# Block-sparse attention with an MLP behind it: the queues that carry P through DRAM

## The chip, the cores and the metric

The kernel runs on one core of a Trainium2 chip. The metric is the device time of one execution in microseconds, lower is better. The kernel before was timed three times: the median is 821.48 us (818.59 to 822.83).

## What is computed

Attention over 4 batches, 8 heads, 768 positions and head size 64, in blocks of 32 positions. A query block sees its neighbours, the first and the last block and three sampled blocks; the first and the last query block see everything. The heads are then joined to rows of 512 and pass a two-layer MLP.

```python
scores = scale * np.matmul(q, k.transpose(0, 1, 3, 2))
scores = np.where(mask, scores, -1000000000.0)
attn = np.exp(scores - np.max(scores, axis=-1, keepdims=True))
attn = attn / (np.sum(attn, axis=-1, keepdims=True) + 1e-09)
x = np.matmul(attn, v)            # [B, H, S, D] -> [B * S, H * D]
h = x @ w_in                      # 3072 x 512 by 512 x 2048
return (h * (1.0 / (1.0 + np.exp(-1.702 * h)))) @ w_out
```

## The kernel before

Tokens go through in six chunks of 512. The MLP of a chunk runs in 16 ticks, one for each 128 columns of the hidden layer (`tick`, L800). A tick holds the first product (`up`, L613: lines 624 to 626), the gate (`gate`, L629: tanh on ScalarE in line 632, a product on VectorE in line 641), its split into a high and a low part (line 648 on ScalarE, line 656 on VectorE) and the second product of the tick before (`down`, L659: lines 682, 686, 687). While one chunk's MLP runs, the attention of the next chunk is done in the gaps. The second weight lies split in DRAM (`ws`); each tick `stream` (L597) loads one piece of it through SyncE into one of two `wst` buffers (line 601), and `split` (L603) makes its two parts by a cast on ScalarE (line 606) and a subtraction on VectorE (line 607).

Attention is cut into items. A sparse item is two query blocks of all heads; a dense item is half of the heads against half of the keys of the first and last query block. `plan` (L740) places each item on quarters of ticks: its scores at one quarter (lines 306 or 318 on TensorE, the minimum in line 329 on VectorE, the exponentials in line 344 on ScalarE), its product with the values later (line 413 for sparse, 435 for dense items). In the sparse stretches some 15 quarters lie between the two, in the dense ones 8, and dense items follow each other every 4 quarters.

For the product with the values P has to be turned. 42 items (28 sparse, 14 dense) are marked `moved`: their exponentials stay in PSUM, VectorE turns them in squares of 32 into the only `ex` buffer (`turned_blocks`, line 356, two instructions), and `move` (L359) brings the squares to their places: one DMA from `ex` to one of two DRAM buffers `way` (line 365), and four DMAs from there to a `raw` buffer (line 367), each 32 partitions. The reads wait for the landing of the write. `pop` (L372) runs these three steps, either inside `gate`, just ahead of line 641, or at the end of a tick, just ahead of `split`.

Each engine issues its DMAs in the order in which the program writes them, and an instruction that waits holds what is behind it on that engine. SyncE issues nearly all of them: query and key loads (lines 206 to 218; the sampled key blocks in line 229, each with its block number read into a register first, line 228), values (lines 236 to 253), the weight pieces (line 601), the output (line 712) and P's five. GpSimd issues the gathers of sampled values (line 258) and, in the first chunk, the raw weights (line 517). ScalarE issues next to none.

Of the kernel before, what the change touches and what calls it, by code (L numbers as in the profile page):

```python
# [20 lines left out]
BLK = 32  # L21
# [29 lines left out]
class Kernel:  # L51
# [307 lines left out]
    def move(self, g):  # L359

        nt = 4 if self.sparse(g) else 3
        n = 2 * nt * BLK
        to = self.work.tile([P, 2 * DM], I32, name="raw", bufs=3).bitcast(F32)[:, 0:4 * n].rearrange("p (c f) -> p c f", c=4)
        way = self.way[g["n"] % 2][:, 0:4 * n]
        self.nc.sync.dma_start(out=way, in_=g["st"])
        for r in range(4):
            self.nc.sync.dma_start(out=to[BLK * r:BLK * (r + 1)],  # L367
                                   in_=way[:, n * r:n * (r + 1)].rearrange("(c i) f -> i c f", c=4))
        pt = to.rearrange("p c (h k j) -> p h k c j", h=2, k=nt)
        g["pt"] = [pt[:, h] for h in range(2)]  # L370

# [628 lines left out]
```

## Time and profile before

| | |
|---|---|
| median of three runs | 821.48 us (818.59 to 822.83) |
| the profiled execution, its own time | 815.69 us |
| its span | 813.9 us |
| TensorE (PE) busy | 723.9 us, 89% |
| VectorE (DVE) busy | 450.4 us, 55% |
| ScalarE (ACT) busy | 341.1 us, 42% |
| GpSimd (POOL) busy | 69.8 us, 9% |
| DMA engines, SyncE's queue | 49.9% of 16 engines' span |
| DMA engines, GpSimd's queue | 14.9% |

All times are of one execution. The first chunk's attention fills the span up to some 160 us, ticks with moved items run from 160 to 704 us, and the last chunk's MLP stands alone behind that. Busy time of TensorE includes products that run at the lower of its two clock levels. An engine's wait is named by what ended last. Times after an instruction's start are its duration; a DMA has besides a time from its issue to its landing.

### The profile page before, as it was taken

The numbers are of one execution on the slowest core, as the hardware profiler recorded it, in microseconds if no ns is written. First come the engines' busy times: TensorE is split into PE (matmuls) and PEld (weight loads), VectorE is DVE, ScalarE is ACT, GpSimd is POOL, SyncE is SP. The second block draws the span as 40 slices with busy tenths as digits, with TensorE's granted clock in tenths as the row PEclk, the third lists the DMA queues.
The fourth block names the chain that finished last, engine by engine and source line by source line (L and its number), as shares of the span: only waits on it lengthen the run. The fifth ranks groups of instructions, "written<-read, shape, count | busy, mean of one in ns | idle before, by whom it ended". The sixth has DMA issues, their size and how long they took to land.

```text
span 813.9 us, 19176 instructions
## 1 busy us (share of the span) xinstructions
PE 723.9 (89%) x7452; PEld 542.8 (67%) x7452; DVE 450.4 (55%) x1153; ACT 341.1 (42%) x855; POOL 69.8 (9%) x111
## 2 busy tenths in 40 slices
PE   3879999999797978979988888899896999999997
PEld 2665667766575746757666666667574767788885
DVE  4669888985563544535643636544564647443332
ACT  4656666754242423423433425233442434333322
POOL 5323211011000001000000000100000000000000
PEclk9999999999898989989999998999998999999999
DMA  8999976767776669676766466666667766441111
GB/s 259 283 370 375 323 268 237 246 198 231 215 242 201 184 202 266 199 203 212 225 203 207 123 191 214 212 197 214 198 195 252 248 193 195 138 103 40 52 52 52
DMA packets 94492, 167.28 MB, mean 206 GB/s; under 512 B 10977, under 2 KB 55266, under 8 KB 93890
## 3 DMA queue, kind: packets, MB, share of 16 engines
q1 hardware_dynamic: 82162, 124.10, 49.9%
q0 software_dynamic: 11376, 41.03, 14.9%
q8 instruction: 59, 0.97, 0.5%
q10 hardware_dynamic: 864, 0.93, 0.3%
q14 instruction: 31, 0.25, 0.1%
HBM read 135.34 MB, written 30.67 MB: 204 GB/s over the span
## 4 chain that ended last, share of the span: by engine, by line
PE 42%; DMA 20%; SPq 14%; DVE 11%; ACT 7%; issue 6%; ACTq 0%; DVEq 0%
DMA way<-ex 10%; PE bank L624 6%; DMA wst<-ws 6%; PE bank L625 6%; PE bank L626 6%; PE bank L682 4%; PE bank L686 4%; PE bank L687 4%; ACT bank L344 4%; SPq L228 4%; SPq L229 3%; PE bank L671 3%; PE bank L306 3%; SPq L367 2%; PE bank L413 2%
## 5 line engine op out<-in xcount | busy, mean ns | idle before, releaser
L686 PE MATMUL bank<-wout,ghi 128*128 128x512 f32 x352 | 139.0, 395 | 0.0
L687 PE MATMUL bank<-wout,ghi 128*128 128x512 f32 x352 | 137.1, 390 | 0.0
L607 DVE TENSOR_TENSOR wout<-wst,wout 128x512 fp32r<-128x512 f32 x80 | 55.1, 688 | 137.6 <-ACT wout L606 136.2
L632 ACT ACTIVATE g<-bank 128x512 f32<-128x512 f32 x96 | 57.5, 599 | 142.0 <-PE bank L626 142.0
L682 PE MATMUL bank<-wout,glo 128*128 128x512 f32 x352 | 100.3, 399 | 17.2 <-DVE glo L656 17.1
L641 DVE SCALAR_TENSOR_TENSOR g<-g,bank 128x512 f32<-128x512 f32 x83 | 56.1, 676 | 89.1 <-ACT g L632 89.0
L344 ACT ACTIVATE bank<-bank,nm 128x256 f32<-128x256 f32 (+1 forms) x140 | 65.3, 467 | 94.3 <-DVE nm L329 89.0
L648 ACT CAST ghi<-g 128x512 fp32r<-128x512 f32 x88 | 54.4, 618 | 97.6 <-DVE g L641 97.6
L624 PE MATMUL bank<-x,win 128*128 128x512 f32 x192 | 80.9, 421 | 14.2 <-DVE g L641 14.2
L624 PE MATMUL bank<-xhi,win 128*128 128x512 f32 x192 | 80.9, 421 | 11.3 <-DVE g L641 10.7
L682 PEld LDWEIGHTS bank<-wout,glo 128*128 128x128 f32 x352 | 66.3, 191 | 35.0 <-DVE glo L656 20.6
L329 DVE CUSTOM_DVE_ANT_1 bank<-bank,bias 128x256 f32<-128x256 f32 x176 | 73.6, 440 | 21.1 <-PE bank L306 14.5
L625 PE MATMUL bank<-x,win 128*128 128x512 f32 x192 | 78.0, 406 | 0.0
L626 PE MATMUL bank<-x,win 128*128 128x512 f32 x192 | 77.7, 405 | 0.0
L258 POOL DMA_INDIRECT vown<-in_v_dram,vidx x40 | 39.8, 994 | 433.9 <-PE bank L413 309.4
L625 PE MATMUL bank<-xlo,win 128*128 128x512 f32 x192 | 76.5, 398 | 0.0
L626 PE MATMUL bank<-xhi,win 128*128 128x512 f32 x192 | 76.4, 398 | 0.0
L686 PEld LDWEIGHTS bank<-wout,ghi 128*128 128x128 f32 x352 | 66.2, 188 | 13.8
L687 PEld LDWEIGHTS bank<-wout,ghi 128*128 128x128 f32 x352 | 66.2, 188 | 13.4
L606 ACT CAST wout<-wst 128x512 fp32r<-128x512 f32 x80 | 49.3, 616 | 59.5 <-DMA wst<-ws 59.5
L356 DVE STREAM_TRANSPOSE ex<-bank 128x512 f32<-128x512 f32 (+1 forms) x84 | 51.8, 651 | 35.8 <-DMA way<-ex 33.4
L306 PE MATMUL bank<-kg,qt 64*32 64x256 f32 x1280 | 49.3, 414 | 12.8 <-DMA vmid<-in_v_dram 11.5
(151 smaller groups left out, 1030.6 us busy)
## 6 DMA issues: line engine op xcount, KB each, us to landing
wst<-ws SPq DMA_DIRECT2D x80, 256.0 KB, 3.2
kg<-in_kb_dram SPq DMA_DIRECT2D x114, 128.0 KB, 2.7
way<-ex SPq DMA_DIRECT2D x28, 512.0 KB, 4.0
raw<-way SPq DMA_DIRECT2D x112, 128.0 KB, 2.9
kg<-in_kb_dram SPq DMA_DIRECT2D x42, 256.0 KB, 4.5
win<-in_moe_w_in_dram POOLq DMA_DIRECT2D x16, 512.0 KB, 7.4
raw<-in_moe_w_out_dram POOLq DMA_DIRECT2D x16, 512.0 KB, 5.9
kg<-in_kT_dram SPq DMA_DIRECT2D x4, 1536.0 KB
```

Of the source, the lines that this page charges most:

```text
L306: nc.tensor.matmul(sps[h][BLK * c:BLK * (c + 1), n * i:n * (i + 1)].rearrange("p (g n s) -> p g n s", g=2, s=BLK), self.qt[r][rows, bi, UT ...
L329: nc.vector.tensor_tensor_reduce(out=at, in0=at, in1=bias, scale=-SCALE, scalar=3.0e38, op0=ALU.add, op1=ALU.min, accum_out=un["nm"][:, ha ...
L344: nc.scalar.activation(out=ex, in_=sps[h][:, n * k:n * (k + 1)], func=AF.Exp, bias=un["nm"][:, half, c:c + 1], scale=-1.0, accum_out=un["r ...
L607: self.nc.vector.tensor_tensor(out=t[:, DM:2 * DM], in0=w, in1=t[:, 0:DM].bitcast(F32), op=ALU.subtract)
L624: nc.tensor.matmul(to, wih[:, k], xh, start=(k == 0), stop=False)
L625: nc.tensor.matmul(to, wih[:, k], xl, start=False, stop=False)
L626: nc.tensor.matmul(to, wil[:, k], xh, start=False, stop=(k == NCT - 1))
L632: nc.scalar.activation(out=g, in_=self.h, func=AF.Tanh, scale=0.851)
L641: nc.vector.scalar_tensor_tensor(out=g, in0=g, scalar=1.0, in1=h, op0=ALU.add, op1=ALU.mult)
L682: nc.tensor.matmul(to[n], glo[:, tk[n]], woh, start=False, stop=last)
L686: nc.tensor.matmul(to[n], ghi[:, tk[n]], woh, start=(f == 0), stop=False)
L687: nc.tensor.matmul(to[n], ghi[:, tk[n]], wol, start=False, stop=False)
```

## The change

The DMA from `ex` to `way` is issued by ScalarE, and the four from `way` to `raw` by GpSimd. Sizes, buffers and the place in the program stay.

```diff
         way = self.way[g["n"] % 2][:, 0:4 * n]
-        self.nc.sync.dma_start(out=way, in_=g["st"])
+        self.nc.scalar.dma_start(out=way, in_=g["st"])
         for r in range(4):
-            self.nc.sync.dma_start(out=to[BLK * r:BLK * (r + 1)],
-                                   in_=way[:, n * r:n * (r + 1)].rearrange("(c i) f -> i c f", c=4))
+            self.nc.gpsimd.dma_start(out=to[BLK * r:BLK * (r + 1)],
+                                     in_=way[:, n * r:n * (r + 1)].rearrange("(c i) f -> i c f", c=4))
```

On SyncE, behind the stores of a finished chunk, the order changes in this way (`out` is the output, `ws` and `wst` the weight pieces, `qt` and `kg` queries and keys):

```order
 L712 DMA out_dram<-raw 64x512 x4
 L712 DMA out_dram<-a 64x512 x4
-L365 DMA way_85<-ex 128x1024
-L367 DMA raw<-way_85 32x4x256 x4
 L601 DMA wst<-ws_72 128x512
 L601 DMA wst<-ws_73 128x512
-L365 DMA way_86<-ex 128x1024
-L367 DMA raw<-way_86 32x4x256 x4
 L206 DMA qt_105<-in_qd_dram 128x256
 L207 DMA kg_103<-in_kT_dram 128x3072
```

P's five DMAs no longer stand between the stores, the weight pieces and the next keys, and no wait for P's landing does.

On ScalarE, at the same place, the changed kernel has these rows in a row:

```order
L726 ACTIVATE a<-bank_92 128x512
L365 DMA way_85<-ex 128x1024
L606 CAST wout<-wst 128x512
L632 ACTIVATE g<-bank_94 128x512
L648 CAST ghi<-g 128x512
L606 CAST wout<-wst 128x512
L344 ACTIVATE bank_87,rs<-bank_87,nm 128x256 x2
L344 ACTIVATE bank_88,rs<-bank_88,nm 128x256 x2
L491 CAST xhi_110<-bank_89 128x4x64
L632 ACTIVATE g<-bank_94 128x512
L365 DMA way_86<-ex 128x1024
L648 CAST ghi<-g 128x512
```

The write stands once ahead of the cast of a weight piece (a `pop` at a tick's end) and once between tanh and the cast of the gate (a `pop` inside `gate`). Of the 42 writes 27 stand ahead of line 648, 8 ahead of line 606, 4 ahead of line 491 (the cast of the turned attention output), 2 ahead of line 452 (the dense items' factors) and 1 ahead of line 539.

On GpSimd, from the last raw weight on, the reads take turns with the gathers (`vown`):

```order
L517 DMA raw<-in_moe_w_out_dram 128x1024
L367 DMA raw<-way_85 32x4x256 x4
L258 DMA vown_107<-in_v_dram,vidx 128x1024 x2
L367 DMA raw<-way_86 32x4x256 x4
L367 DMA raw<-way_85 32x4x256 x4
L367 DMA raw<-way_86 32x4x256 x4
L258 DMA vown_106<-in_v_dram,vidx 128x1024 x2
```

Before, the gathers stood there alone; a gather now waits behind reads that wait for a write's landing.

## Rows read from the trace of the kernel before

**Rows 1.** Waits of TensorE, 160 to 704 us (us in total, times, longest)

```profile
PE bank L624 <- DVE g L641: 24.9, 12, 6.2
PE bank L682 <- DVE glo L656: 17.1, 6, 6.1
PE bank L435 <- DMA raw<-way: 8.0, 5, 2.8
PE bank L318 <- DVE ex L356: 7.5, 2, 4.7
PE bank L484 <- DVE x L492: 2.3, 1, 2.3
```

**Rows 2.** The first of these by stretch: 160 to 320, 320 to 600, 600 to 710 us

```profile
PE bank L624 <- DVE g L641: 8.8, 3, 5.8
...
PE bank L624 <- DVE g L641: 9.3, 7, 3.5
...
PE bank L624 <- DVE g L641: 6.8, 2, 6.2
```

**Rows 3.** Waits in SyncE's queue, 160 to 710 us, the longest

```profile
SPq L367 <- DMA way<-ex: 191.2, 42, 11.1
```

**Rows 4.** Waits of ScalarE, 160 to 710 us, the one for weights

```profile
ACT wout L606 <- DMA wst<-ws: 59.5, 14, 11.0
```

**Rows 5.** Timelines of SyncE and TensorE, a late weight piece (start, duration, instruction, idle before)

```profile
338.17 1.75 SPq L367 DMA_DIRECT2D raw<-way  x4
...
342.15 6.38 SPq L229 DMA_DIRECT2D kg<-in_kb_dram  x6
...
354.02 2.01 SPq L601 DMA_DIRECT2D wst<-ws  x2
...
361.41 2.08 PE L682 MATMUL bank<-wout,glo 128*128 128x512 f32 x4 [5.71 <-DVE glo L656]
```

**Rows 6.** Timelines of SyncE, VectorE and TensorE, a late write of P

```profile
199.88 0.56 SPq L365 DMA_DIRECT2D way<-ex  x1
...
205.46 1.31 DVE L356 STREAM_TRANSPOSE ex<-bank 128x512 f32<-128x512 f32 x2 [3.89 <-DMA way<-ex]
...
207.40 0.79 PE L624 MATMUL bank<-x,win 128*128 128x512 f32 x1 [5.84 <-DVE g L641]
```

**Rows 7.** Windows: PE, PEld, DVE, ACT, POOL busy (instructions), TensorE clock, DMA share, GB/s

```profile
160.00:704.00 544.00, 480.74 (x5155) 359.66 (x5154) 286.61 (x735) 208.63 (x538) 25.50 (x26) 0.95 0.68 208
206.00:208.00 2.00, 0.60 (x2) 0.51 (x3) 1.35 (x3) 0.62 (x1) 0.00 (x0) 0.50 0.65 189
```

**Rows 8.** Timelines of TensorE and VectorE, dense items 640 to 697 us

```profile
640.52 0.88 PE L318 MATMUL bank<-kg,qt 64*64 64x384 f32 x8
...
644.19 1.04 DVE L356 STREAM_TRANSPOSE ex<-bank 128x384 f32<-128x384 f32 x2
...
696.00 0.88 PE L318 MATMUL bank<-kg,qt 64*64 64x384 f32 x8
```

**Rows 9.** Lines 229 and 258: issue on GpSimd and ScalarE (duration ns min/median/max, starts)

```profile
L229 ACTq DMA_DIRECT2D kg<-in_kb_dram x3: 354/355/378, 3.1 to 5.3; - x3
...
L229 POOL DMA_DIRECT2D kg<-in_kb_dram x3: 536/571/727, 5.0 to 7.4; - x3
...
L258 POOL DMA_INDIRECT vown<-in_v_dram,vidx x40: 933/939/1438, 12.3 to 605.6; - x40
```

**Rows 10.** DMA issues: engine, count, KB each, median us to landing

```profile
way<-ex SPq DMA_DIRECT2D x28, 512.0 KB, 4.0
raw<-way SPq DMA_DIRECT2D x112, 128.0 KB, 2.9
...
kg<-in_kb_dram POOLq DMA_DIRECT2D x3, 128.0 KB, 4.2
...
wout<-in_kb_dram POOLq DMA_DIRECT2D x3, 128.0 KB, 8.9
```

**Rows 11.** Costliest groups: gate product (busy us, mean ns, idle before, releaser)

```profile
L641 DVE SCALAR_TENSOR_TENSOR g<-g,bank 128x512 f32<-128x512 f32 x83 | 56.1, 676 | 89.1 <-ACT g L632 89.0
```

## The prediction

> **What bounds the kernel now.** I read the waits of TensorE first. From 160 to 704 us it is busy for 480.74 of 544 us [rows 7], so 63.3 us are waits, and five rows hold 59.8 of them [rows 1] (two of under 2.5 us are left out there: another wait for the turned attention output, one for an exponential). None names the DMA queues except the 8.0 us of dense items for `raw`, so the next views are the timelines behind the longest waits, to see what made VectorE late. There are two patterns.
>
> *A weight piece comes late.* SyncE issues P's reads until 339.92 us, then six sampled key blocks, then a finished chunk's stores, and only at 354.02 the weight piece; the cast, the subtraction and the low part of the gate follow it, and TensorE stands for 5.71 us [rows 5]. ScalarE waited 59.5 us in 14 such places [rows 4]. To this I count the waits for line 656 but two of 1 us (17.1 - 2 = 15), for line 492 (2.3 and its like of 2.2, [rows 1]) and the longest of the middle stretch for line 641 (3.5, [rows 2]): **23 us**.
>
> *P's write comes late.* Line 356 may not overwrite `ex` before the last write has left it. At 199.88 us that write is issued behind a chunk's stores, the next turning waits 3.89 us for it, line 641 stands behind that, and TensorE behind line 641 for 5.84 us [rows 6]. With it go its like of 6.2 us in the last stretch [rows 2] and the two waits for line 356, 7.5 us [rows 1]: **19.5 us**.
>
> The reads themselves make 8.0 us [rows 1]. The rest, 63.3 - 23 - 19.5 - 8.0 = 12.8 us, are waits of 1 to 2 us for an item's own chain (scores, exponentials, turning, line 641); no queue is in it.
>
> Behind both patterns stands SyncE: it waits 191.2 us in 42 moves for P's landing [rows 3], 4.55 us each, and everything behind it waits too.
>
> **The change part by part.**
>
> *Off SyncE.* Each move takes 4.55 us of waiting, 1.75 us for four reads [rows 5] and 0.4 to 0.56 us for the write [rows 6]: 6.7 us, 42 times, 281 of 544 us. A piece that was late by what TensorE then waited (at most 6.1 us, [rows 1]) comes 6.7 us earlier where one move stood ahead of it. So I take 20 of the 23 us as gone; where keys and stores together still fill the two ticks for which a `wst` buffer lasts, the wait stays: bounds 10 to 23.
>
> *The write on ScalarE's queue.* It leaves when the turning ends, not behind stores or keys, and lands on a queue that holds nothing else. Of the 19.5 us the four places keep what the item's own chain costs elsewhere, some 1.3 us each: 14.3 us gone, bounds 8 and 19.5.
>
> *What it costs ScalarE.* The issue is 0.355 us on that queue [rows 9], and ScalarE stands until line 356 has ended. In 27 of 42 places the next instruction is the cast of line 648, which waits for line 641 anyway, and that one comes behind line 356 on VectorE and takes 0.676 us [rows 11]: the wait and the issue lie beside it and cost nothing. If line 641 came first, the cover would be gone and each of the 27 would cost up to 1.04 us of turning [rows 8] and the issue. In the other 15 places a cast or factor that could go at once is held for up to 1.04 + 0.36 + 0.2 us (the 0.2 for handing over, my estimate from 1.75 us for four issues of SyncE [rows 5], whose gaps are smaller): 24 us at most, 0 at least, since ScalarE is busy for 208.63 of 544 us [rows 7]. I take a third, 8 us, because the instruction that follows on VectorE stands behind the turning too, and only the cast's own time comes on top.
>
> *What it costs GpSimd.* 168 issues by 0.571 us [rows 9] are 96 us on an engine that is busy for 25.50 of 544 us [rows 7]. Gathers stand behind reads, by a write's landing of 4.0 us [rows 10] and 2.3 us of issues; they fill a buffer that is used only after two more items, some 30 quarters, which hides it. Without that cover it would be 6 us for each of the gathers' pairs.
>
> *The reads' landing.* No row shows a read of `way` by GpSimd. From below 2.9 us, as by SyncE, from above 8.9 us, a 128 KB load by GpSimd in the crowded prelude; 4.2 us is another of the same size there [rows 10]. I take 5, near the lower of GpSimd's own rows, for traffic in the stage is thinner. It counts in the dense stretches only: sparse items have 15 quarters. There items follow each other by (696.00 - 640.52) / 7 = 7.9 us, and an item's values come two items later, behind the scores of that one: 2 x 7.9 + 0.9 = 16.7 us [rows 8]. Its chain is 4.7 us to the end of the turning (645.23 - 640.52, [rows 8]), 0.4 for the issue, 4.0 for the write, 2.3 for four issues on GpSimd, 5 for the landing: 16.4 us. It just fits. Each us more would cost half a us for each of 14 dense items. So I leave the 8.0 us where they are: a write that leaves earlier and reads that take longer. Bounds: a gain of 8, or (8.9 - 5) / 2 x 14 = 27 us lost.
>
> The Trainium skill ("DMA: Bandwidth & Descriptors", section "Latency and other measured facts") puts the first byte at about 1 us on GpSimd's path against 0.6 on the other: by that the reads would land at about 3.3 us, and the dense items would gain a little instead.
>
> *The clock.* It falls to half, 1.2 GHz, behind long waits (0.50 in 206 to 208 us, [rows 7], with the wait of [rows 6] ahead of it). A mean of 0.95 over 544 us [rows 7] is 2 x 0.05 x 544 = 54 us at the lower level. Where TensorE worked in that time, half of it is lost; with a third of it spent waiting (in 206 to 208 it is 70%, later less, an estimate) that is 18 us. The two patterns are 42.5 of 63.3 us and hold all long waits, so I take 13 back: bounds 0 and 25.
>
> *The sum*: -20 - 14.3 + 8 - 13 = **-39 us**. The profiled execution took 815.69 us; it would take 776.4. The median of the three runs is 5.8 us above that execution, so I predict 821.48 - 39 = **782 us**. A measurement of this kernel can tell some 0.5% from no change, 4.1 us.
>
> **The rivals.**
>
> *The waits only change their name* (chance 0.17). With weights and writes in time, TensorE runs into each item's own chain, which stands in DVE's and ACT's order whatever the queues do. For it speaks that 12.8 us of such waits are there now and that the long ones hide others. If each of 42 moves then waits 0.6 us more than now, 25 us come back: 39 - 25 = 14, about **807 us**. Against it: at 640 to 697 us, where SyncE has no keys to load, items run at 7.9 us with hardly a wait [rows 8].
>
> *The queues are not the point* (0.09). If P's landing is bounded by the engines that move it, another queue only saves issue time on SyncE, 42 x 2.2 = 92 us that lie beside other work: no gain, **821 us**. For it: the DMA share is 0.68 over the stage [rows 7]. Against it: SyncE's wait, not the issue, is the larger part [rows 3], and key loads and stores stand behind it in program order. This is the rule of the Trainium skill ("DMA: Bandwidth & Descriptors", section "Issuing engines are not separate DMA queues"): all transfers end on the same DMA engines, and spreading the issue saves only the sequencer's time, usually little beside the transfer. The trace agrees that the engines are shared and cannot show more; the rule leaves out what an in-order queue holds back.
>
> *Slower: GpSimd's reads land late and dense items wait for them* (0.11). With 12 us to the landing, the chain is 23.4 us, the spacing (23.4 - 0.9) / 2 = 11.3 instead of 7.9, and 14 items lose 48 us; the 7.5 us of line 356 and some 4 us of clock are not won either: 782 + 48 + 11 = **841 us**. It decides from the point where 14 items lose the 39 us, 2.8 us each, at a landing of 5 + 2 x 2.8 = 10.6 us. For it: 8.9 us was seen [rows 10]. Against it: that was ahead of the stage, and the gathers' issue on GpSimd holds at 939 ns (median) with a greatest of 1438 [rows 9], so nothing starves that engine. The Trainium skill has a mechanism for it ("SBUF — State Buffer", section "SBUF: two separate sides"): while VectorE copies or casts in its two-port mode, GpSimd cannot write descriptors and its DMAs seem blocked. VectorE's large instructions here are of other kinds, and the steady 939 ns agrees.
>
> **How the numbers follow.** The forecast has 0.63, with its own range of 762 to 802 us from the bounds (not all at one end). The first rival still is faster. Faster: 0.63 + 0.17 = 0.80; same 0.09; slower 0.11. The range must hold 8 in 10: from 760, where weights, writes and clock all give their upper bounds, to 814, which takes in the first rival and leaves out the other two.
>
> **What would show it.** Right: no long wait in SyncE's queue for `way`; ScalarE's 59.5 us for weights below 15; the turning's wait for `way` nearly gone; TensorE busy for over 92% of the stage, at a clock of 0.97 or more; line 648 no later behind line 641 than now. Wrong: long waits of line 435 for `raw` (the reads), casts of line 606 held by the write, or waits of 5 us and more that stay for another reason. A landing of GpSimd's reads above 10 us would overturn the sign.

## The result, and the profile after

The changed kernel takes **772.79 us** (median of four, 772.28 to 776.03) against 820.39 us before (median of four, 818.59 to 822.83): a ratio of **0.943**, 95% interval 0.939 to 0.946, 47.6 us less. Forecast were 782 us and 39 us less, with a range of 760 to 814.

The span of the profiled execution is 770.6 us instead of 813.9. Ticks with moved items now end at 662 us instead of 704. The row of the windows view for that stage (columns as in [rows 7]):

```profile
160.00:662.00 502.00, 467.88 (x5186) 355.15 (x5188) 289.72 (x741) 209.54 (x537) 119.05 (x194) 0.98 0.74 226
```

Against [rows 7], TensorE's waits fell from 63.3 to 502 - 467.88 = 34.1 us, 29 us less, and its busy time from 480.74 to 467.88 us, 13 us less for the same products: that is the clock, 0.98 in the mean instead of 0.95 (480.74 x 0.95 and 467.88 x 0.98 are 457 and 459 us). Together they are 42 of the 43.3 us by which the span shrank. GpSimd is busy for 119 us instead of 25.5, which no wait of TensorE shows.

What TensorE still waits for, 160 to 665 us (us in total, times, longest), answers to [rows 1]:

```profile
PE bank L413 <- DMA raw<-way: 12.9, 4, 4.4
PE bank L624 <- DVE g L641: 6.8, 6, 3.0
PE bank L682 <- DVE glo L656: 5.5, 3, 2.3
PE bank L413 <- issue: 4.0, 11, 0.5
PE bank L435 <- DMA raw<-way: 3.0, 4, 1.2
```

The waits for lines 641 and 656 went from 42.0 us to 12.3, and those for line 356 and line 492 are gone. New is a row that was not there: sparse items' products (line 413) wait for P itself, 12.9 us. A second profile of the changed kernel has the same rows with 10.1 us for line 413, 9.5 and 6.4 us for lines 641 and 656, and 6.7 us for line 435.

The waits of SyncE's queue, of ScalarE for weights, of VectorE for the write and of GpSimd for P's landing, in the same stretch, answer to [rows 3], [rows 4] and [rows 6]. Four views:

```profile
SPq L601 <- DVE wout L607: 253.1, 45, 12.0
SPq L601 <- DMA wst<-ws: 16.9, 9, 3.2
```

```profile
ACT wout L606 <- DVE ex L356: 10.9, 6, 2.1
ACT wout L606 <- DMA wst<-ws: 5.4, 4, 3.8
```

```profile
DVE ex L356 <- DMA way<-ex: 5.0, 3, 2.9
```

```profile
POOL raw L367 <- DMA way<-ex: 285.4, 31, 19.8
```

SyncE still waits for more than 250 us, but at another place: it stands ahead of a weight piece whose buffer is not yet free, so it is early where it was late. ScalarE's wait for weight pieces fell from 59.5 to 5.4 us. In its place stand 10.9 us of line 606 for the turning: the write that now stands ahead of it on ScalarE. The wait for P's landing has not gone, it is GpSimd's now.

How the write costs ScalarE nothing in most places is seen at 199 us, in the timelines of ScalarE and of VectorE:

```profile
199.22 0.60 ACT L632 ACTIVATE g<-bank 128x512 f32<-128x512 f32 x1 [1.09 <-PE bank L626]
199.84 0.33 ACTq L365 DMA_DIRECT2D way<-ex  x1
200.57 0.62 ACT L648 CAST ghi<-g 128x512 fp32r<-128x512 f32 x1 [0.75 <-DVE g L641]
```

```profile
198.50 1.30 DVE L356 STREAM_TRANSPOSE ex<-bank 128x512 f32<-128x512 f32 x2
199.85 0.69 DVE L641 SCALAR_TENSOR_TENSOR g<-g,bank 128x512 f32<-128x512 f32 x1
```

The write leaves at 199.84, as the turning ends, and its issue of 0.33 us lies beside line 641, for which the cast waits anyway.

### The profile page after: what moved, and what is told of

Same layout as the page of the kernel before. It is cut to its first block, busy times and chain, and to the rows that moved or that the text cites. A ratio compares the mean times of both kernels' runs of the same rounds, so it can differ in the third digit from the quotient of the medians.

```text
span 770.6 us, 19301 instructions
## 1 busy us (share of the span) xinstructions
PE 712.1 (92%) x7452; PEld 535.7 (70%) x7452; DVE 452.5 (59%) x1153; ACT 341.7 (44%) x855; POOL 163.3 (21%) x279
## 4 chain that ended last, share of the span: by engine, by line
PE 52%; DMA 18%; DVE 11%; ACT 9%; issue 5%; SPq 2%; POOL 2%; ACTq 0%; POOLq 0%; DVEq 0%
PE bank L624 8%; PE bank L625 8%; PE bank L626 8%; DMA raw<-way 7%; PE bank L682 6%; PE bank L687 6%; PE bank L686 6%; DMA way<-ex 5%; PE bank L413 3%; PE bank L306 3%; ACT bank L344 3%; PE bank L671 2%; DVE ex L356 2%; POOL raw L367 2%; DVE bank L329 2%
## 5 line engine op out<-in xcount | busy, mean ns | idle before, releaser
L367 POOL DMA_DIRECT2D raw<-way x168 | 93.0, 564 | 376.6 <-DMA way<-ex 285.4
L624 PE MATMUL bank<-xhi,win 128*128 128x512 f32 x192 | 79.8, 416 | 4.6 <-DVE g L641 4.0
L624 PE MATMUL bank<-x,win 128*128 128x512 f32 x192 | 78.3, 408 | 2.8 <-DVE g L641 2.8
L625 PE MATMUL bank<-x,win 128*128 128x512 f32 x192 | 75.6, 394 | 0.0
L626 PE MATMUL bank<-xhi,win 128*128 128x512 f32 x192 | 75.5, 393 | 0.0
L626 PE MATMUL bank<-x,win 128*128 128x512 f32 x192 | 75.5, 393 | 0.0
L656 DVE TENSOR_TENSOR glo<-g,ghi 128x512 fp32r<-128x512 f32 x88 | 60.2, 684 | 0.7 <-ACT ghi L648 0.7
L606 ACT CAST wout<-wst 128x512 fp32r<-128x512 f32 x80 | 49.2, 615 | 20.4 <-DVE ex L356 10.9
```

The source lines that it names most:

```text
L367: self.nc.gpsimd.dma_start(out=to[BLK * r:BLK * (r + 1)], in_=way[:, n * r:n * (r + 1)].rearrange("(c i) f -> i c f", c=4))
L624: nc.tensor.matmul(to, wih[:, k], xh, start=(k == 0), stop=False)
L625: nc.tensor.matmul(to, wih[:, k], xl, start=False, stop=False)
L626: nc.tensor.matmul(to, wil[:, k], xh, start=False, stop=(k == NCT - 1))
L656: self.nc.vector.tensor_tensor(out=glo, in0=g, in1=ghi.bitcast(F32), op=ALU.subtract)
```

## The experiments

**Theory A** is the prediction's: what costs is SyncE standing until P has landed, with keys, stores and weight pieces behind it. **B**: the write needs a queue of its own. **C**: SyncE's issue time is what was saved. D and E concern the new row of line 413. Each ratio is against runs of the kernel before on the same chip.

### The two halves of the change

Reads to GpSimd, write left on SyncE (against the changed kernel):

```diff
-        self.nc.scalar.dma_start(out=way, in_=g["st"])
+        self.nc.sync.dma_start(out=way, in_=g["st"])
```

> Only the four reads go to GpSimd; the write of P stays on SyncE. Theory A (what counts is SyncE standing until P has landed, with keys, stores and weight pieces behind it): the 20 us for late weight pieces are gained with most of the clock's 13, the late writes' 14 are not: 783 to 795 us, and waits of line 356 for the write stay above 20 us. Theory B (what counts is that the write has a queue of its own): 805 us or more. Theory C (only SyncE's issue time counts, 1.75 of 2.2 us a move are taken off): most of the gain, 773 to 785 us.

Measured: 784.82 us, ratio 0.953 (0.942 to 0.963). B falls. The time lies in A's range and, at the upper end, in C's as well; the runs below decide between the two. One part of the expectation failed: line 356 waits 0.2 us for the write, not over 20. Waits of SyncE, TensorE and VectorE in this run, 160 to 690 us:

```profile
SPq L365 <- DVE ex L356: 149.8, 36, 9.1
SPq L601 <- DVE wout L607: 115.4, 41, 9.8
```

```profile
PE bank L413 <- DMA raw<-way: 18.9, 5, 6.7
...
PE bank L435 <- DMA raw<-way: 7.6, 1, 7.6
```

```profile
DVE ex L356 <- DMA way<-ex: 0.2, 1, 0.2
```

Once SyncE no longer stands for the landing, it mostly reaches the write in time even on its own queue: it waits there for the turning, and 36 of the 42 writes leave within 0.1 us of its end. The other six leave 2.5 to 5.4 us late, two of them behind a chunk's eight stores, such as this one, whose turning ended at 191.75 (timeline of SyncE):

```profile
194.46 2.48 SPq L712 DMA_DIRECT2D out_dram<-a  x4
197.17 0.40 SPq L365 DMA_DIRECT2D way<-ex  x1
```

This write and one at 276 us, 2.9 us late behind keys, values and a weight piece, stand at the head of the two longest waits for `raw`, 6.7 and 7.6 us. All of these are 26.5 us instead of 15.9 (16.8 in the second profile of the changed kernel). The late writes are a part of the difference; how large a part is not shown, for two more of the long waits (3.0 and 3.7 us) follow writes that left at once.

Write to ScalarE, reads left on SyncE (against the kernel before):

```diff
-        self.nc.sync.dma_start(out=way, in_=g["st"])
+        self.nc.scalar.dma_start(out=way, in_=g["st"])
```

> Only the write goes to ScalarE; SyncE keeps the reads and the wait ahead of them. Theory A: 795 to 812 us, SyncE's wait for the landing still above 120 us, late weight pieces still there (ScalarE above 30 us for them). Theory B: 775 to 790 us. Theory C: only 0.4 us of issue a move is taken off, 815 us or more.

Measured: 808.33 us, ratio 0.987 (0.975 to 0.998). This is A's range and not B's. SyncE and ScalarE wait as before:

```profile
SPq L367 <- DMA way<-ex: 218.3, 35, 12.3
```

```profile
ACT wout L606 <- DMA wst<-ws: 61.4, 13, 15.6
```

### The wait without a new queue, and the issues without the wait

All five on SyncE as before, the reads two quarters later in the program:

```diff
         self.nc.sync.dma_start(out=way, in_=g["st"])
+        self.pending.append((self.quarter, lambda: self.fetch(g, way, nt, n)))
+
+    def fetch(self, g, way, nt, n):
...
         for r in range(4):
             self.nc.sync.dma_start(out=to[BLK * r:BLK * (r + 1)],
...
     def begin(self, q):
 
+        self.quarter = q
+        while self.pending and q - self.pending[0][0] >= 2:
+            self.pending.pop(0)[1]()
```

> All five stay on SyncE as before; the reads are written two quarters of a tick (some 4.4 us) later in the program, so that the write has mostly landed when SyncE comes to them. Issue time and queue are as before. Theory A: SyncE's wait for the landing falls from 191 us to below 60 and most of the weights' share comes: 783 to 800 us. Theories B and C: no gain, 815 us or more.

Measured: 775.53 us, ratio 0.944 (0.935 to 0.953): as good as the change and better than A's range, with no engine and no queue added. SyncE's waits from 160 to 665 us (line 370 holds the reads here) and TensorE's from 160 to 690 us (416 is 413 of before):

```profile
SPq L604 <- DVE wout L610: 72.8, 30, 6.4
SPq L364 <- DVE ex L356: 70.3, 29, 5.9
SPq L370 <- DMA way<-ex: 46.2, 21, 4.3
```

```profile
PE bank L416 <- DMA raw<-way: 19.2, 10, 3.7
```

The wait for the landing is 46 us instead of 191; a quarter of it is left. B and C would have given nothing.

Five small loads more on SyncE at the place of P's five, into the columns of a buffer that no one reads:

```diff
+        for r in range(5):
+            self.nc.sync.dma_start(out=self.pad[:, 8 * r:8 * (r + 1)], in_=self.q[:, 0, 0, 8 * r:8 * (r + 1)])
```

> The changed kernel with five small loads more on SyncE in each of the 42 moves, at the place where P's five stood, that nothing waits for: some 1.8 us of issue back on that queue and no wait. Theory A: 773 to 781 us. Theory C: the gain goes, 795 us or more.

Measured: 773.59 us, ratio 0.936 (0.924 to 0.949). 210 issues put back on SyncE cost nothing that can be measured: C falls. The loads were not quite without waits: SyncE stood ahead of them (line 367 here, 160 to 690 us) for some 47 us, at most 5.5 at a time, and that cost nothing either.

```profile
SPq L367 <- DMA kg<-in_kT_dram: 19.7, 4, 5.5
SPq L367 <- DMA kg<-in_kb_dram: 13.8, 8, 4.3
SPq L367 <- DMA pad<-in_q_dram: 13.2, 11, 4.4
```

The opposite, one small read of `way` on SyncE, which waits for the landing; the change stays otherwise:

```diff
+        self.nc.sync.dma_start(out=self.pad[:, 8 * (g["n"] % 7):8 * (g["n"] % 7) + 8], in_=way[:, 0:8])
```

> The changed kernel with one small read of P's DRAM buffer (32 bytes a partition) put on SyncE in each move, at the place where the four reads stood: it waits for P's landing and issues one transfer that nobody waits for. So the wait alone is back on SyncE, with a sixth of the issues. Theory A: most of the gain of the weights and of the clock goes, 795 to 812 us, SyncE waits over 120 us for the write. Theory C (issue time): 773 to 778 us.

Measured: 812.43 us, ratio 0.990 (0.981 to 0.998), just above the expected range. The wait alone, which is even longer here than the 191 us of before, takes back most of what the change gave. SyncE and ScalarE, 160 to 690 us:

```profile
SPq L366 <- DMA way<-ex: 261.7, 35, 13.1
```

```profile
ACT wout L607 <- DMA wst<-ws: 52.7, 11, 9.2
```

### The same wait on other engines

Write and reads on ScalarE:

```diff
-            self.nc.gpsimd.dma_start(out=to[BLK * r:BLK * (r + 1)],
+            self.nc.scalar.dma_start(out=to[BLK * r:BLK * (r + 1)],
```

> Write and reads on ScalarE, GpSimd as before the change. The wait for the landing, some 4 us in each of 42 moves, and 1.4 us of issues then hold an engine that TensorE waits for through the gate. Theory A in its general form (a wait for a transfer costs what stands behind it on that engine): slower than the changed kernel by 50 us or more and about as slow as the kernel before or slower, 815 to 900 us. If ScalarE's idle time hid it: below 790 us.

Measured: 923.96 us, ratio 1.128 (1.119 to 1.136), above the upper end of what was expected. ScalarE's casts come late and TensorE waits for them (160 to 665 us); the clock falls to 0.91 in the mean of the span. ScalarE has the 168 issues of the reads as well, 0.44 us each in the median or some 74 us, so this run does not tell the wait's share from theirs.

```profile
PE bank L686 <- ACT ghi L648: 41.0, 14, 5.7
PE bank L682 <- DVE glo L656: 35.2, 9, 6.4
```

All five on GpSimd:

```diff
-        self.nc.scalar.dma_start(out=way, in_=g["st"])
+        self.nc.gpsimd.dma_start(out=way, in_=g["st"])
```

> All five of P's transfers on GpSimd, which then waits for the turning, for the landing and issues all. Theory A (any queue helps that holds nothing TensorE needs soon, and ScalarE's hold of 8 us comes back): within 1% of the changed kernel, 765 to 785 us, ScalarE without waits of line 606 for line 356. Theory B (the write needs one of the hardware queues of its own, ScalarE's): 790 us or more.

Measured: 775.01 us, ratio 0.941 (0.934 to 0.947), beside the changed kernel's own second measurement:

> The changed kernel once more, beside the three that follow on the same chip: 0.94 of the kernel before, 768 to 785 us.

Measured: 771.96 us, ratio 0.938 (0.933 to 0.943). The two cannot be told apart, and B falls once more. Line 606 no longer waits for the turning, as expected. GpSimd's standing does little harm, because only P and the gathers are behind: TensorE waits for a gather 0.9 us in one profile of the changed kernel and not at all in the other.

### The new row: P late for sparse items

In the changed kernel the reads at 229 us land after 11.5 us. The chain of waits (start, us, what), and the timeline of SyncE at that time:

```profile
224.38 2.61 DMA way<-ex
...
227.56 1.62 POOL raw L367 x3
229.19 11.49 DMA raw<-way
240.68 0.14 issue
240.81 1.25 PE bank L413 x37
```

```profile
227.04 0.36 SPq L207 DMA_DIRECT2D kg<-in_kT_dram  x1
227.88 0.32 SPq L236 DMA_DIRECT2D vown<-in_vd_dram  x1
```

1.5 MB of dense keys and 0.75 MB of values are issued within a microsecond of the first of the reads. So the keys were loaded in parts:

```diff
-            nc.sync.dma_start(out=self.kg[r].rearrange("p n b c -> p (n b c)"), in_=self.kT[b])
+            flat = self.kg[r].rearrange("p n b c -> p (n b c)")
+            part = lambda i, n: nc.sync.dma_start(out=flat[:, S * i:S * (i + n)], in_=self.kT[b][:, S * i:S * (i + n)])
+            part(0, 2)
+            self.later = [lambda: part(2, 1), lambda: part(3, 1)]
...
         self.stream(m + 3)
+        if self.later:
+            self.later.pop(0)()
```

> The changed kernel with the 1.5 MB load of a dense unit's keys in three parts, half at once and two quarters one tick each later. In the changed kernel line 413 waited 12.9 us for P in four places, three of them with the reads issued within 2 us of such a load and landing after 10.7 to 11.6 us. Theory D (the bulk on SyncE's queue takes the DMA engines from the reads): landings of 5 to 8 us there, line 413 below 5 us, 5 to 10 us faster than the changed kernel. Theory E (GpSimd's reads are late by themselves): no difference.

Measured: 762.89 us, ratio 0.925 (0.920 to 0.931) beside 0.938 for the changed kernel on the same chip: 9 us faster, as D said. TensorE's waits for P in this run's profile (160 to 665 us, 416 and 438 are 413 and 435 of before) are not what D said:

```profile
PE bank L438 <- DMA raw<-way: 8.4, 5, 3.5
PE bank L416 <- DMA raw<-way: 8.2, 6, 1.7
```

Line 416 waits less than line 413 did, but line 438 more, and the sum is 16.6 us, no less than the 15.9 and 16.8 of the changed kernel. A second measurement, beside other runs of the kernel before:

> The dense keys in three parts once more, beside the next kernel: 755 to 767 us, 0.92 to 0.93 of the kernel before.

Measured: 766.52 us, ratio 0.936 (0.929 to 0.944), which alone would not tell it from the changed kernel. In the chains of both runs no read takes 10 us; the longest takes 7.2 us (two of the second run below). Line 416 waits 1.7 us at most instead of 4.4, but keeps 8.5 us in all, not below 5:

```profile
211.18 6.38 DMA raw<-way
240.59 4.38 DMA raw<-way
```

```profile
PE bank L416 <- DMA raw<-way: 8.5, 6, 1.7
...
PE bank L438 <- DMA raw<-way: 4.4, 4, 2.2
```

All waits for P are 12.9 us here; a third profile with keys in parts, that of the last run below, has 14.2. The clock of 160 to 660 us is 0.99 in all three instead of 0.98. So D is borne out for the long landings and not for the waits: three measurements with GpSimd's reads and the keys in parts (0.925, 0.936, 0.934, the last with the write moved) lie below the two of the changed kernel (0.943, 0.938), but where the 6 to 9 us come from these profiles do not show, beyond the clock.

Both remedies with other queues, write on ScalarE, reads two quarters later on SyncE, keys in parts:

> Write on ScalarE, reads on SyncE two quarters later in the program, dense keys in three parts, GpSimd as in the kernel before. Theory A: the reads wait nowhere long, so this is as good as the changed kernel or better by up to 10 us (760 to 778 us). Theory E: better than the changed kernel by the whole of line 413's 12.9 us. A rival: the reads come 4 us later and dense items wait for them, 785 us or more.

Measured: 771.49 us, ratio 0.939 (0.934 to 0.945): as good as the change, not better, and behind the run with parts alone (0.925) on the same chip. Its reads come later, and line 413 (419 here) waits 16.5 us for them, so E's gain did not come, though the time by itself does not test E's cause. A read in this run's chain does, and so does one in the chain of the run with the reads later and the keys whole:

```profile
227.38 10.99 DMA raw<-way
```

```profile
227.65 9.26 DMA raw<-way
```

Both are issued by SyncE, behind half of the keys or all of them and 0.75 MB of values, and land as late as GpSimd's. So it is not GpSimd that makes them late, against E; and half of the keys beside values can still do it, against a simple reading of D.

### ScalarE's hold

With keys in parts, the write behind the cast in the 8 places where it held line 606:

```diff
+        move = []
         if late:
...
+            move = self.blocks.pop()
             self.pop()
         self.split(m + 1)
+        if move:
+            move()
```

> Dense keys in three parts, and in the 8 places where the write of P stood ahead of the cast of a weight piece on ScalarE, the write behind it. In the run with parts ScalarE waited 15.0 us there for the turning. If ScalarE's hold costs time (the prediction put 8 us on 15 such places): 3 to 6 us faster than the run with parts. If it is hidden: within 2 us of it.

Measured: 766.30 us, ratio 0.934 (0.927 to 0.941), beside 766.52 us without it. In that neighbour ScalarE waits this long for the turning (line 609 is 606 before), and here the row is gone:

```profile
ACT wout L609 <- DVE ex L359: 10.9, 6, 2.1
```

The medians are 0.2 us apart, but the intervals (some 1% each) are wider than the 3 to 6 us in question. That the hold lies in time that ScalarE had to spare is likely and not shown.

## Why the prediction was right

**What bounds the kernel** was right and is now shown by runs: the wait for P's landing at the head of SyncE's queue. Taking three quarters of it away without another engine gives 0.944, putting it back alone gives 0.990, putting the issues back with little of it gives 0.936. The signs that the prediction named came too: ScalarE's wait for weights is below 15 us, TensorE is busy for 93% of the stage, and line 648's wait for line 641 fell from 80.7 to 58.0 us. The clock's share followed: 13 us were forecast and 13 us of TensorE's busy time went.

**The sum** of waits came near (-26 forecast, -29 measured), in part by luck. Line 413 brought 16.9 us (12.9 for P, 4.0 without a named cause) that the sum did not have. They were made up by terms that came out better: the waits for lines 641, 656, 356 and 492 fell from 54.0 us to 12.3, 7.4 more than forecast, ScalarE's 8 us are not seen, and the dense items' reads gave 5.0. About half of the 8.6 us between 39 and 47.6 lies in the executions that are compared: the profiled one of before is 4.7 us under its median and the changed kernel's only 0.5. Term by term:

- *Off SyncE*, 20 us for late weight pieces. ScalarE's wait for them fell by 54 us (48 in the second profile), TensorE's for line 656 from 17.1 to 5.5 us, and that for line 492 is gone. Right.
- *The write on ScalarE's queue*, 14.3 us: the late writes went, but this queue was not needed for it. VectorE's wait for the write, 160 to 704 us, was in the kernel before

```profile
DVE ex L356 <- DMA way<-ex: 33.4, 13, 8.3
```

  and is 5.0 us with the change, 0.2 with the reads alone moved, 6.2 with the write alone moved. Either half takes it away: the writes were late for the most part because SyncE stood for the landing of the write before. Beyond that the write's own queue gives some 1% between the two runs (0.953 and 0.943, intervals that touch), and 1.3% by itself with the wait left in place.
- *What it costs ScalarE*, 8 us: over-estimated, as far as can be told. The covered places are covered as at 199 us. In 6 of the 8 places ahead of line 606 the wait is there (10.9 us), and without it the time is the same to 0.2 us, within intervals that are wider than the term.
- *The reads' landing*, 5 us taken. The second profile of the changed kernel shows 5.1 us for 128 KB and 4.3 us for 96 KB reads (columns as in [rows 10]):

```profile
raw<-way POOLq DMA_DIRECT2D x112, 128.0 KB, 5.1
...
raw<-way POOLq DMA_DIRECT2D x56, 96.0 KB, 4.3
```

  The size is right, and the dense items' waits for reads fell from 8.0 to 3.0 us (6.7 in the second profile). Its reason, GpSimd's queue, is not borne out. The same reads with all five on SyncE, later in the program, and with the reads alone on GpSimd:

```profile
raw<-way SPq DMA_DIRECT2D x112, 128.0 KB, 4.1
```

```profile
raw<-way POOLq DMA_DIRECT2D x112, 128.0 KB, 3.9
```

  On SyncE they take 4.1 us where the kernel is as fast as the change, on GpSimd 3.9 to 5.1. What sets them apart from the 2.9 us of before [rows 10] is then not the queue; the stage is more crowded (a DMA share of 0.74 to 0.76 instead of 0.68), and whether that is the cause was not tested. The 3.3 us in the prediction were an estimate from the first byte's about 1 us on GpSimd's path against 0.6 on the other, which the Trainium skill states ("DMA: Bandwidth & Descriptors", section "Latency and other measured facts"). The measured 3.9 to 5.1 us are above it, and no run here shows the first byte by itself.
- *"It counts in the dense stretches only: sparse items have 15 quarters"*: wrong. That holds for chunks without dense units. In the two chunks that have them the plan puts the sparse items 5 or 6 quarters apart, and their values come 10 or 11 quarters after the scores. With reads that land after 11 us beside the dense keys, that was not enough: 12.9 us (10.1 in the second profile) that the sum did not have.

**The rivals.** That the waits only change their name happened in small part: lines 641 and 656 together kept 12.3 us (15.9 in the second profile), about the 12.8 us that were put down to the items' own chain, and the new waits of line 413 are such a change of name, but not the 25 us of the rival. That the queues are not the point holds in a sense that it did not mean: no new queue is needed, as the reads later on SyncE show. But it is not the issue time that is saved either; it is the standing. That all transfers end on the same engines, which is the rule of the Trainium skill that the rival named ("DMA: Bandwidth & Descriptors", section "Issuing engines are not separate DMA queues"), agrees with reads that land as late by either queue beside the dense keys (9.3 to 11.6 us). The slower rival named the right danger: landings of 10.7 to 11.6 us, beyond its point of 10.6 us, did occur, but beside bulk loads, in a few places and by either queue, and nothing held GpSimd up (issues of the reads on it take 0.550 to 0.627 us throughout).

## What to carry to other kernels

An instruction that waits for a transfer holds everything behind it in its engine's queue, so ask of each wait what stands behind it, not which engine is free: the wait cost 40 us on SyncE, nothing that could be measured on GpSimd and, with the issues of the reads, 151 us against the change on ScalarE. Before moving transfers to another engine, try to write the dependent half later in the program, where it has already landed; here that alone gave the whole gain. And a megabyte issued beside small reads that are needed soon may be worth cutting into parts: it shortened the landings here, and the time by some 1%.

## What had not been expected of the hardware

- A large load lengthens small reads that are issued beside it, on another queue or on its own: 128 KB reads by GpSimd took 10.7 to 11.6 us to land where 1.5 MB of keys (and in two places 0.75 MB of values) were issued at about the same time on SyncE, and 5.1 us in the median; reads by SyncE itself took 9.3 us behind such loads and 11.0 us behind half of the keys and the values. With the keys in parts GpSimd's longest read in the chain took 7.2 us in one run, 6.4 in another and 8.6 in a third. How much the reads lose was not foreseen.
